# A fused attention and FFN kernel on one core: buffers relaid so that FFN weights lie over attention buffers, first FFN LayerNorm inside attention, wo over two banks, last tile in column pieces

## Chip, cores, metric

One Trainium2 chip, one of its cores. The metric is the device time of one execution of the program, in microseconds (us); the kernel before ran three times: 936.22, 937.30 and 937.99 us, median 937.3.

## What is computed

Two branches share a normalised input xn (2048 rows of 576), in bf16. Branch A is attention of 32 heads against a cached K and V of 16 heads (the last 512 positions of the cache). Branch B is a small mixer and an FFN. The result joins both.

```python
xn = layernorm(x)
q  = (xn @ wq)                       # 32 heads of 128
s  = softmax(q k^T / sqrt(128)) v @ wo
h  = gelu(layernorm(xn) @ w1)        # 576 to 576
x1 = xn + shifted(h) @ w2            # four column groups, shifted by +1 -1 +2 -2 rows
b  = x1 + gelu(layernorm(x1) @ w3) @ w4   # 576 to 4608 to 576
out = x + s * silu(b)
```

## The kernel before

The rows are split into four query blocks of 512. The first half of the program is the attention. It runs over 128 units, a unit being one head of one block. In the turn of unit u TensorE (PE) does four stages: `stage_q` (L268) projects q of unit u+1 over five chunks of 128 input columns, `stage_s` (L283) makes the scores of unit u in four chunks, whose exponentials ACT writes as pT (L285), `stage_v` (L298) multiplies pT of unit u-1 with v into two PSUM banks called po, from which VectorE (DVE) makes the reciprocal ri (L301) and the normalised o (L302), and `stage_t` (L309) has a DMA transpose on SP's queue turn o of unit u-2 into oT. The buffers of o are three (`o_pool`), those of oT 36.

Everything else is hung on unit numbers in a table `fill`: the output projection wo of the block before (`wo_units`, L325 for 512 columns of each row tile, L336 for the other 64 of all four tiles), the second LayerNorm (`ln2`) and its transposes (`tr2`, L239, into xnnT), the mixer's matmuls `b1` (L363) and `b2` (L399, result x1o by L404 and L410, stored to x1_dram by L411), the LayerNorm of the next block (`ln1`), loads of K and V (`load_kv`, L180 and L181) and of wq in pieces of four heads (`load_wq`, L175 and L177), and a check on the size of the scores. For the check DVE takes the largest absolute value of each K head (`k_max`, L256) and of each wq piece (L470, one reduction over 2560 columns), and `finish_flag` sends the maxima through a small DRAM tile mx_dram to one partition (L416 to L425). A branch at the end of the program would redo the attention in a safer form if the flag were set; it isn't taken. The last block's wo runs after the last unit, alone on PE, over the one bank of `ps_wo`.

The second half is the FFN. It loads x1 of a block (L519), normalises it (`ln3`: L116, L117, L95 to L105, L120, written to xm_b) and transposes it by DMA (L535) into x1nT; the weights w3 and w4 come in nine slices (`load_w`, L525 to L529, all of them tiles w_s in the profile). For each block of rows it runs 36 steps of `up` (L558, with the gelu on ACT at L561) and of `down` (L567 for 512 columns into one of four banks pm, L568 for 64 columns into pr). `finish` then makes the output of each of four tiles: bs (L576, L577), tanh (L579), g (L581, stored to g_dram by POOL at L582, which only the fallback branch reads), o (L584, L585) and the store (L586). The last block does all its ups first and then its downs tile by tile, so that three finishes lie beside matmuls.

The Python order of the calls isn't the order on each engine. A scheduler reorders independent instructions, so a load or a reduction may be issued long before its place in the program; `manual_schedule(engines=...)` and `keep_in_program_order` turn that off for the engines or instructions named. Each engine then runs its own list strictly in order, DMA issues included. SBUF is given out in stacks of pools: pools of the second half lie where pools of the first half lay, in order of their declaration, and a tile's first write waits until the readers of whatever lay there are done.

Of the kernel before, what the change touches and what calls it, by code (L numbers as in the profile page):

```python
# [8 lines left out]
P = 128  # L9
# [6 lines left out]
SP = mybir.EngineType.SP  # L16

# [10 lines left out]
def kernel(  # L28
# [94 lines left out]

    with ExitStack() as actx:
# [5 lines left out]
        wo_sb = res.tile([P, Hq, D], BF16, name="wo_sb")  # L130
# [4 lines left out]
        xnT_b = [res.tile([P, NDC, QB], BF16, name=f"xnT_b{i}") for i in range(2)]  # L135
        xnnT = res.tile([P, NDC, QB], BF16, name="xnnT")
        xn_b = [res.tile([P, TB, DP], BF16, name=f"xn_b{i}") for i in range(2)]
        xnn_b = res.tile([P, TB, DP], BF16, name="xnn_b")
        w1_sb = res.tile([P, NDC, 5 * P], BF16, name="w1_sb")
        w2_sb = res.tile([P, 5, D], BF16, name="w2_sb")  # L140
        mx = res.tile([P, 8 + Hkv], FP32, name="mx")
        gate = res.tile([1, 1], BF16, name="gate")

        oT_pool = pool("oT_pool", 36)
# [3 lines left out]
        o_pool = pool("o_pool", 3)  # L148
# [92 lines left out]
        def tr1_first():  # L241
            for kc, (cst, cw) in enumerate(DCH):
# [19 lines left out]
        def stage_q(u):  # L262
# [51 lines left out]
        def wo_units(qb):  # L314
            units = []
            st = {}
            for tt in range(TB):
                for h0 in range(0, Hq, 8):
                    def unit(tt=tt, h0=h0):
                        if tt == 0 and h0 == 0:  # L320
                            so_t[qb] = so_pool.tile([P, TB, D], BF16, name="s_out")
                        if h0 == 0:
                            st["ps"] = ps_wo.tile([P, M0], FP32, name="pswo", tag="wo")
# [7 lines left out]
            for tt in range(TB):  # L331
                def unit(tt=tt):
                    if tt == 0:
                        st["pr"] = ps_wo.tile([P, TB, R0], FP32, name="pswr", tag="wo")
# [46 lines left out]
        x1_t = {}  # L381

        def b2_shift(b):
# [6 lines left out]
            x1_t[b] = x1o_pool.tile([P, TB, D], BF16, name="x1o")  # L390
# [347 lines left out]
```

## Time and profile before

| | value |
|---|---|
| median of three runs | 937.3 us |
| the profiled execution's own time | 935.56 us |
| its span, first to last instruction | 933.7 us |
| mean granted TensorE clock | 0.982 |
| PE busy | 860.9 us (92%) |
| DVE, ACT, POOL busy | 376.5 (40%), 433.4 (46%), 46.0 (5%) us |
| DMA, mean over the span | 90 GB/s |

The span is read from left to right as follows: a start of some 12 us in which PE has nothing, the attention up to 577 us, the last block's wo to 611, a junction, and the FFN from 625 to the end. PE is the engine with the most work, so the places where PE stands still, and those where its granted clock is below full speed, are what an edit can win.

### The profile page before, as it was taken

How to read it: one execution, taken by the hardware profiler on the slowest of the kernel's cores; microseconds unless marked ns; L12 is line 12 of the kernel's file. 1: busy time of each engine (PE TensorE's matmuls, PEld its weight loads, DVE VectorE, ACT ScalarE, POOL GpSimd, SP SyncE). 2: the span in 40 equal slices, each digit the busy share in tenths (PEclk: the TensorE clock that was granted, in tenths of full speed). 3: DMA queues.
4: the chain of work that ended last, by engine and by line, in shares of the span. 5: the costliest groups of instructions: out<-in, count | busy, mean ns of one | idle time of the engine just before them, and what ended most of it. 6: DMA issues, size and time to landing. Idle time of an engine off the chain costs nothing.

```text
span 933.7 us, 15814 instructions
## 1 busy us (share of the span) xinstructions
PE 860.9 (92%) x6266; PEld 469.7 (50%) x6376; DVE 376.5 (40%) x1180; ACT 433.4 (46%) x812; POOL 46.0 (5%) x93
## 2 busy tenths in 40 slices
PE   4799889999969999999999999939999999999996
PEld 2455545554545465555465555424444444444453
DVE  7769763348743226563116543300306006003022
ACT  2556553366657247677247665013224224224510
POOL 1501200000000000000000000010000000000000
PEclk9999999999999999999999999979999999999998
DMA  8975952132463123274123234279105004101001
GB/s 183 208 169 138 196 107 55 53 90 60 104 118 91 37 69 88 58 153 113 16 69 86 60 86 106 87 224 311 30 1 148 9 1 127 29 1 51 0 15 41
DMA packets 162960, 83.72 MB, mean 90 GB/s; under 512 B 119488, under 2 KB 160704, under 8 KB 162880
## 3 DMA queue, kind: packets, MB, share of 16 engines
q1 hardware_dynamic: 159184, 72.16, 33.4%
q0 software_dynamic: 3408, 10.19, 4.1%
q8 instruction: 52, 0.85, 0.4%
q10 hardware_dynamic: 288, 0.30, 0.1%
q14 instruction: 28, 0.23, 0.1%
HBM read 47.07 MB, written 9.44 MB: 61 GB/s over the span
## 4 chain that ended last, share of the span: by engine, by line
PE 69%; issue 13%; ACT 9%; DMA 5%; DVE 3%; SPq 1%; POOL 0%; DVEq 0%; ACTq 0%; POOLq 0%
PE ph L558 16%; PE pm L567 13%; PE psq L268 11%; PE pswo L325 10%; PE po L298 7%; PE sc L283 6%; ACT qT L274 4%; ACT pT L285 4%; PE pr L568 2%; PE ph L363 2%; DMA oT<-o 2%; PE psx L399 1%; DMA kT<-in_A_k_cache_dram 1%; PE pswr L336 1%; DMA wq_b<-in_A_wq_dram 1%
## 5 line engine op out<-in xcount | busy, mean ns | idle before, releaser
L285 ACT ACTIVATE pT<-sc 128x512 bf16<-128x512 f32 x512 | 266.1, 607 | 58.1 <-PE sc L283 58.0
L558 PE MATMUL ph<-x1nT,w_s 128*128 128x512 bf16 x701 | 173.5, 383 | 15.1 <-DMA x1nT<-xm_b 14.0
L298 PEld LDWEIGHTS <-pT 128*128 128x128 bf16 x2048 | 140.9, 99 | 91.3 <-DVE o L302 27.1
L298 PE MATMUL po<-v_sb,pT 128*128 128x129 bf16 x2048 | 164.4, 222 | 21.3 <-DVE o L302 21.3
L561 ACT ACTIVATE h<-ph 128x512 bf16<-128x512 f32 x144 | 85.6, 596 | 171.7 <-PE ph L558 171.6
L283 PE MATMUL sc<-qT,kT 128*128 128x512 bf16 x512 | 153.4, 381 | 6.6 <-ACT pT L285 0.9
L268 PE MATMUL psq<-xnT_b,wq_b 128*128 128x512 bf16 x600 | 156.3, 386 | 2.3 <-issue 0.2
L567 PE MATMUL pm<-w_s,h 128*128 128x512 bf16 x557 | 152.2, 380 | 0.2
L301 DVE RECIPROCAL ri<-po 128x2 f32<-128x2 f32 x256 | 42.4, 167 | 194.5 <-PE po L298 193.3
L302 DVE TENSOR_TENSOR o<-po,ri 128x256 bf16<-128x256 f32 x256 | 107.5, 422 | 17.4 <-DMA oT<-o 11.2
L325 PE MATMUL pswo<-wo_sb,oT 128*128 128x512 bf16 x497 | 111.8, 379 | 2.8 <-ACT s_out L328 2.1
L558 PEld LDWEIGHTS <-w_s 128*128 128x128 bf16 x720 | 64.3, 99 | 89.4 <-DMA x1nT<-xm_b 14.1
L568 PE MATMUL pr<-w_s,h 128*128 128x64 bf16 x576 | 108.0, 193 | 1.0
L274 ACT ACTIVATE qT<-psq 128x512 bf16<-128x512 f32 x96 | 57.3, 597 | 78.3 <-PE psq L268 78.1
L576 DVE TENSOR_TENSOR bs<-pm,x 128x512 f32<-128x512 f32 x16 | 10.7, 687 | 204.8 <-PE pm L567 149.8
L567 PEld LDWEIGHTS <-h 128*128 128x128 bf16 x576 | 56.2, 98 | 67.3
L268 PEld LDWEIGHTS <-wq_b 128*128 128x128 bf16 x640 | 60.2, 99 | 58.6 <-issue 3.5
L325 PEld LDWEIGHTS <-oT 128*128 128x128 bf16 x512 | 49.4, 98 | 59.7 <-issue 2.9
L283 PEld LDWEIGHTS <-kT 128*128 128x128 bf16 x512 | 50.4, 99 | 46.2 <-issue 1.8
L568 PEld LDWEIGHTS <-h 128*128 128x128 bf16 x576 | 55.4, 98 | 12.7
L328 ACT ACTIVATE s_out<-pswo 128x512 bf16<-128x512 f32 x16 | 9.6, 597 | 105.4 <-PE pswo L325 105.4
L116 DVE BATCH_NORM_STATS2 ln_st<-x 128x6 f32<-128x288 bf16 x32 | 12.5, 431 | 71.9 <-DMA x<-x_dram 71.9
(83 smaller groups left out, 419.3 us busy)
## 6 DMA issues: line engine op xcount, KB each, us to landing
wq_b<-in_A_wq_dram SPq DMA_DIRECT2D x32, 512.0 KB, 3.9
w_s<-in_B_w_dram SPq DMA_DIRECT2D x9, 576.0 KB, 8.2
wo_sb<-in_A_wo_dram POOLq DMA_DIRECT2D x4, 1152.0 KB, 8.0
w_s<-in_B_w_dram SPq DMA_DIRECT2D x9, 512.0 KB, 8.4
s_dram<-s_out SPq DMA_DIRECT2D x4, 576.0 KB, 3.3
x_dram<-x1o SPq DMA_DIRECT2D x4, 576.0 KB, 3.3
s_b<-s_dram SPq DMA_DIRECT2D x4, 576.0 KB, 5.5
x_b<-in_A_x_dram SPq DMA_DIRECT2D x4, 576.0 KB, 6.3
```

The costliest lines, as they stand in the source:

```text
L268: nc.tensor.matmul(psq[:, :], lhsT=w[:, kc, hh * Dh:(hh + 1) * Dh], rhs=xnT_b[qb % 2][:, kc, :], start=(kc == 0), stop=(kc == NDC - 1))
L274: nc.scalar.activation(out=qT[:, :], in_=psq[:, :], func=ACT.Copy)
L283: nc.tensor.matmul(sc[:, :], lhsT=kT[:, g, kc * P:(kc + 1) * P], rhs=qT[:, :], start=True, stop=True)
L285: nc.scalar.activation(out=pT[:, :], in_=sc[:, :], func=ACT.Exp, scale=SCALE)
L298: nc.tensor.matmul(po[:, j, :], lhsT=pTs[kc][:, tt * P:(tt + 1) * P], rhs=v_sb[:, g, kc, 0:Dh + 1], start=(kc == 0), stop=(kc == KCH - 1))
L301: nc.vector.reciprocal(out=ri[:], in_=po[:, :, Dh])
L302: nc.vector.tensor_tensor(out=o[:, t0:t0 + 2, :], in0=po[:, :, 0:Dh], in1=ri[:].unsqueeze(2).to_broadcast([P, 2, Dh]), op=ALU.mult)
L325: nc.tensor.matmul(st["ps"][:, :], lhsT=oT_t[qb * Hq + h][:, tt, :], rhs=wo_sb[:, h, 0:M0], start=(h == 0), stop=(h == Hq - 1))
L558: nc.tensor.matmul(ph[:, :], lhsT=w3[:, kc, f0:f0 + P], rhs=x1nT[b % 2][:, kc, :], start=(kc == 0), stop=(kc == NDC - 1))
L561: nc.scalar.activation(out=h3[:, :], in_=ph[:, :], func=ACT.Gelu_apprx_tanh)
L567: nc.tensor.matmul(pm[tt][:, :], lhsT=lhsT, rhs=w4[:, fc % WS, 0:M0], start=(fc == 0), stop=(fc == FC - 1))
L568: nc.tensor.matmul(pr[:, tt, :], lhsT=lhsT, rhs=w4[:, fc % WS, M0:D], start=(fc == 0 and tt == 0), stop=(fc == FC - 1), skip_group_check=True)
```

## The change

There are five parts.

1. **Buffers.** xT_b (it takes the places of xnT_b and of x1nT), xn_b, xnn_b, the x1 buffers (now one pool of two for x1o and x1) and the small tiles move into pools that live through both halves. oT and wo_sb move to the end of the attention's stack. So the nine pairs of weight slices lie over kT, v_sb, wq_b, xnnT, w1, w2, mx, xraw, qT, pT, o and hb, and no longer over wo_sb.
2. **LN3 inside the attention.** The x1 load of block 0 is called at unit 106 (`3 * Hq + 10`), its LN3 at unit 123. With the buffers of part 1 the scheduler also moves block 1's x1 load and LN3 there.
3. **Order and the score check.** SP and POOL follow program order in the attention. k_max stays at its units in block 1; each wq maximum becomes five reductions of 512 columns, kept in program order. o has four buffers.
4. **Last wo.** The last block's wo takes its banks from ps_pq (two banks) and not from ps_wo (one); its store goes through ACT's queue.
5. **Finish.** o becomes (th + 1) * t1 with t1 = bs * s, so that g is off its path; g's store moves from POOL's to ACT's queue. The last tile is computed in three column pieces of 288, 192 and 96, each with a bank and a finish of its own.

The diff, cut to what the steps speak of:

```diff
+    keep = ctx.enter_context(tc.tile_pool(name="keep", bufs=1))
+    xT_b = [keep.tile([P, NDC, QB], BF16, name=f"xT_b{i}") for i in range(2)]
+    xn_b = [keep.tile([P, TB, DP], BF16, name=f"xn_b{i}") for i in range(2)]
+    xnn_b = keep.tile([P, TB, DP], BF16, name="xnn_b")
+    x1_pool = ctx.enter_context(tc.tile_pool(name="x1_pool", bufs=2))
...
+    def load_x1(b):
+        x1 = x1_pool.tile([P, TB, D], BF16, name="x1")
+        nc.sync.dma_start(out=x1[:], in_=rows(x1_dram, b * TB, TB))
...
         res = pool("a_res", 1)
-        wo_sb = res.tile([P, Hq, D], BF16, name="wo_sb")
         kT = res.tile([P, Hkv, W], BF16, name="kT")
...
-        oT_pool = pool("oT_pool", 36)
...
-        o_pool = pool("o_pool", 3)
+        o_pool = pool("o_pool", 4)
...
+        oT_pool = pool("oT_pool", 36)
+        wo_sb = pool("a_wo", 1).tile([P, Hq, D], BF16, name="wo_sb")
...
+        def wq_max(j, kc):
+            tc.keep_in_program_order(nc.vector.tensor_reduce(
+                out=mx[:, Hkv + NDC * j + kc:Hkv + NDC * j + kc + 1], in_=wq_b[j % NWQ][:, kc, :], axis=AX.X,
+                op=ALU.max, apply_absolute_value=True))
...
+            psp, tag = (ps_pq, "pq") if qb == NB - 1 else (ps_wo, "wo")
...
-                            st["ps"] = ps_wo.tile([P, M0], FP32, name="pswo", tag="wo")
+                            st["ps"] = psp.tile([P, M0], FP32, name="pswo", tag=tag)
...
-                        nc.sync.dma_start(out=rows(s_dram, qb * TB, TB), in_=so_t.pop(qb)[:])
+                        (nc.scalar if qb == NB - 1 else nc.sync).dma_start(out=rows(s_dram, qb * TB, TB),
+                                                                           in_=so_t.pop(qb)[:])
...
+            for kc in range(NDC):
+                at(Hq + 4 * j + (kc + 1) // 2, lambda j=j, kc=kc: wq_max(j, kc))
+        at(3 * Hq + 10, lambda: load_x1(0))
+        at(3 * Hq + 27, lambda: ln3(0))
...
+        with tc.manual_schedule(engines={SP, POOL}):
+            ln1(0)
...
-        load_x1(0)
-        load_w(0)
-        ln3(0)
-        for i in range(1, NSL):
+        for i in range(NSL):
             load_w(i)
...
-            nc.vector.scalar_tensor_tensor(out=g2[:], in0=th[:], scalar=1.0, in1=bs[:], op0=ALU.add, op1=ALU.mult)
-            nc.gpsimd.dma_start(out=g_dram[t * P:(t + 1) * P, :], in_=g2[:])
-            o = fin.tile([P, D], BF16, name="o")
-            nc.vector.tensor_tensor(out=o[:], in0=g2[:], in1=s_b[:, tt, :], op=ALU.mult)
-            nc.vector.tensor_tensor(out=o[:], in0=o[:], in1=x_b[:, tt, :], op=ALU.add)
-            nc.sync.dma_start(out=out2[t * P:(t + 1) * P, :], in_=o[:])
...
+                nc.vector.tensor_tensor(out=t1[:], in0=bs[:], in1=s_b[:, tt, lo:hi], op=ALU.mult)
+                o = fin.tile([P, n], BF16, name="o")
+                nc.vector.scalar_tensor_tensor(out=o[:], in0=th[:], scalar=1.0, in1=t1[:], op0=ALU.add, op1=ALU.mult)
+                nc.vector.tensor_tensor(out=o[:], in0=o[:], in1=x_b[:, tt, lo:hi], op=ALU.add)
+                nc.sync.dma_start(out=out2[t * P:(t + 1) * P, lo:hi], in_=o[:])
+                g2 = fin.tile([P, n], BF16, name="g2")
+                nc.vector.scalar_tensor_tensor(out=g2[:], in0=th[:], scalar=1.0, in1=bs[:], op0=ALU.add, op1=ALU.mult)
+                nc.scalar.dma_start(out=g_dram[t * P:(t + 1) * P, lo:hi], in_=g2[:])
...
+                cuts = [0, 288, 480, D]
+                for i in range(3):
+                    lo, hi = cuts[i], cuts[i + 1]
+                    ps = pm[TB - 1 - i][:, 0:hi - lo]
+                    for fc in range(FC):
+                        nc.tensor.matmul(ps, lhsT=h3_t[fc][:, tt * P:(tt + 1) * P],
+                                         rhs=w4_s[fc // WS][:, fc % WS, lo:hi], start=(fc == 0), stop=(fc == FC - 1))
+                    finish(b, tt, [([(ps, lo, hi)], lo, hi)])
```

The change moves more than these lines show. Three places stand here; a row is one instruction, or several of one kind with their count, in the order in which the engine runs them.

SP's queue early in block 0, before: loads of K and V for thirteen heads come first, and this is where they end and the first oT appears.

```order
L180 DMA_TRANSPOSE kT<-in_A_k_cache_dram 128x512
L181 DMA v_sb<-in_A_v_cache_dram 128x4x128
L180 DMA_TRANSPOSE kT<-in_A_k_cache_dram 128x512
L181 DMA v_sb<-in_A_v_cache_dram 128x4x128
L180 DMA_TRANSPOSE kT<-in_A_k_cache_dram 128x512
L175 DMA wq_b_76<-in_A_wq_dram 128x4x512
L309 DMA_TRANSPOSE oT<-o 128x4x128
L177 DMA wq_b_76<-in_A_wq_dram 64x512
L181 DMA v_sb<-in_A_v_cache_dram 128x4x128
```

The same queue in the changed kernel, from the load of the fourth head on (L196 and L197 are K and V, L330 is oT, L191 and L193 are wq):

```order
L196 DMA_TRANSPOSE kT<-in_A_k_cache_dram 128x512
L197 DMA v_sb<-in_A_v_cache_dram 128x4x128
L330 DMA_TRANSPOSE oT<-o 128x4x128 x2
L196 DMA_TRANSPOSE kT<-in_A_k_cache_dram 128x512
L197 DMA v_sb<-in_A_v_cache_dram 128x4x128
L330 DMA_TRANSPOSE oT<-o 128x4x128
L191 DMA wq_b_89<-in_A_wq_dram 128x4x512
L193 DMA wq_b_89<-in_A_wq_dram 64x512
L330 DMA_TRANSPOSE oT<-o 128x4x128
```

Before, the first oT stands behind nearly all loads of K and V; now the loads of one head stand between two of them.

SP's queue at the end of the attention, before (L309 is oT, L411 the store of x1o, L546 and L548 loads for finish, L519 the x1 load, L340 the store of the last s_out, L526 to L529 the weights, L535 the transposes of LN3's result):

```order
L411 DMA x_dram<-x1o 128x4x576
L309 DMA_TRANSPOSE oT<-o 128x4x128 x6
L546 DMA s_b<-s_dram 128x4x576
L548 DMA x_b<-in_A_x_dram 128x4x576
L546 DMA s_b<-s_dram 128x4x576
L548 DMA x_b<-in_A_x_dram 128x4x576
L519 DMA x_8974<-x_dram 128x4x576
L340 DMA s_dram<-s_out 128x4x576
L526 DMA w_s_8928<-in_B_w_dram 128x4x512
L528 DMA w_s_8928<-in_B_w_dram 64x512
L529 DMA w_s_8937<-in_B_w_dram 128x4x576
L526 DMA w_s_8929<-in_B_w_dram 128x4x512
```

And in the changed kernel (L434 is the store of x1 of a block, L143 the LN3 transposes, L136 an x1 load, L540 to L543 the weights):

```order
L434 DMA x_dram<-x_8147 128x4x576
L330 DMA_TRANSPOSE oT<-o 128x4x128
L143 DMA_TRANSPOSE xT_b_73<-xnn_b 128x5x128 x4
L330 DMA_TRANSPOSE oT<-o 128x4x128
L136 DMA x_9091<-x_dram 128x4x576
L330 DMA_TRANSPOSE oT<-o 128x4x128 x5
L143 DMA_TRANSPOSE xT_b_74<-xn_b_75 128x5x128
L540 DMA w_s_9015<-in_B_w_dram 128x4x512
L542 DMA w_s_9015<-in_B_w_dram 64x512
L543 DMA w_s_9016<-in_B_w_dram 128x4x576
```

The weights stood behind the store of the last s_out and now stand behind the last oT; four LN3 transposes and an x1 load stand among the last oT.

The new x1 load of block 0, on SP in the changed kernel, around unit 105 (L255 are the transposes of the mixer's input, x_7381 is x1 of block 0):

```order
L330 DMA_TRANSPOSE oT<-o 128x4x128
L255 DMA_TRANSPOSE xnnT<-xnn_b 128x5x128 x4
L330 DMA_TRANSPOSE oT<-o 128x4x128
L136 DMA x_7381<-x_dram 128x4x576
L330 DMA_TRANSPOSE oT<-o 128x4x128 x2
```

And the place on DVE where x_7381 is first read (L322 and L323 make ri and o, two pairs for a unit):

```order
L323 TENSOR_TENSOR o<-po,ri 128x256
L322 RECIPROCAL ri<-po 128x2
L323 TENSOR_TENSOR o<-po,ri 128x256
L322 RECIPROCAL ri<-po 128x2
L323 TENSOR_TENSOR o<-po,ri 128x256
L117 BN_STATS ln_st<-x_7381 128x6 x3
L322 RECIPROCAL ri<-po 128x2
L118 BN_AGGR ln_mv<-ln_st 128x2
L117 BN_STATS ln_st<-x_7381 128x6
L323 TENSOR_TENSOR o<-po,ri 128x256
```

Before, no instruction of LN3 stood on DVE before the last unit's o, and no x1 load on SP before the last oT. Now DVE's queue has LN3's first statistics between the o of two units, and SP's queue has the load behind an oT, four transposes and another oT.

## Rows read from the trace of the kernel before

**Rows 1.** Waits (engine, line, releaser; us in total, times, longest us).
```profile
PE po L298 <- DVE o L302: 21.3, 12, 4.1
...
PE ph L558 <- DMA x1nT<-xm_b: 14.0, 1, 14.0
...
DVE o L302 <- DMA oT<-o: 11.2, 6, 4.5
```

**Rows 2.** Costliest groups: VectorE (busy us, mean ns; idle before, by releaser).
```profile
L470 DVE TENSOR_REDUCE mx<-wq_b 128x1 f32<-128x2560 bf16 x8 | 22.6, 2820 | 18.2 <-DMA wq_b<-in_A_wq_dram 18.2
```

**Rows 3.** Windows (start:end, length, busy us by engine, granted clock, DMA share, GB/s).
```profile
40.00:60.00 20.00, 16.48 (x126) 9.76 (x126) 11.83 (x33) 9.59 (x19) 0.00 (x0) 0.91 0.98 203
260.00:280.00 20.00, 12.89 (x96) 7.75 (x96) 10.18 (x34) 9.67 (x19) 1.69 (x2) 0.91 0.61 104
626.00:630.00 4.00, 4.00 (x10) 1.49 (x10) 0.00 (x0) 0.97 (x2) 0.00 (x0) 0.51 1.01 334
```

**Rows 4.** Timeline of TensorE, end of wo and start of FFN (start, us).
```profile
607.29 3.89 PE L336 MATMUL pswr<-wo_sb,oT 128*128 128x64 bf16 x128 [0.69 <-ACT s_out L328]
625.17 0.59 PE L558 MATMUL ph<-x1nT,w_s 128*128 128x512 bf16 x1 [13.98 <-DMA x1nT<-xm_b]
625.97 6.02 PE L558 MATMUL ph<-x1nT,w_s 128*128 128x512 bf16 x18 [0.22 <-issue]
```

**Rows 5.** Timeline of SP's queue at the junction.
```profile
616.18 7.46 SPq L535 DMA_TRANSPOSE x1nT<-xm_b  x4
```

**Rows 6.** Timeline of VectorE, the first LayerNorm.
```profile
7.75 0.69 DVE L256 TENSOR_REDUCE mx<-kT 128x1 f32<-128x512 bf16 x1 [0.72 <-DMA kT<-in_A_k_cache_dram]
...
9.07 0.68 DVE L256 TENSOR_REDUCE mx<-kT 128x1 f32<-128x512 bf16 x1
```

**Rows 7.** SP's transposes by line: issue ns min/median/max, first and last start.
```profile
L309 SPq DMA_TRANSPOSE oT<-o x128: 1188/1191/2740, 28.6 to 577.6; - x128
...
L239 SPq DMA_TRANSPOSE xnnT<-xnn_b x16: 1201/1250/2787, 42.3 to 413.9; - x16
```

**Rows 8.** DMA issues (count, KB each, median us to landing).
```profile
w_s<-in_B_w_dram SPq DMA_DIRECT2D x9, 576.0 KB, 8.2
...
out_dram<-o SPq DMA_DIRECT2D x16, 144.0 KB, 1.9
```

**Rows 9.** Timeline of TensorE and VectorE at the first FFN block boundary.
```profile
701.64 4.48 PE L558 MATMUL ph<-x1nT,w_s 128*128 128x512 bf16 x20
...
705.96 0.59 PE L567 MATMUL pm<-w_s,h 128*128 128x512 bf16 x2
706.14 0.69 DVE L576 TENSOR_TENSOR bs<-pm,x 128x512 f32<-128x512 f32 x1
```

**Rows 10.** Timeline of SP's queue in block 0.
```profile
5.95 0.58 SPq L181 DMA_DIRECT2D v_sb<-in_A_v_cache_dram  x1
6.58 0.51 SPq L175 DMA_DIRECT2D wq_b<-in_A_wq_dram  x1
...
59.01 12.64 SPq L309 DMA_TRANSPOSE oT<-o  x4
```

**Rows 11.** Landing time of the x1 loads, line 519.
```profile
DMA to landing us min/median/max: 4.6/6.8/9.4
```

**Rows 12.** Costliest groups: VectorE's g and o in finish.
```profile
L581 DVE SCALAR_TENSOR_TENSOR g<-th,bs 128x576 bf16<-128x576 f32 x16 | 11.9, 756 | 5.4 <-ACT th L579 5.2
...
L584 DVE TENSOR_TENSOR o<-g,s_b 128x576 bf16<-128x576 bf16 x16 | 7.0, 455 | 0.2
```

**Rows 13.** Timeline of the last tile, all engines.
```profile
924.47 0.19 PE L568 MATMUL pr<-w_s,h 128*128 128x64 bf16 x1
924.67 0.69 DVE L576 TENSOR_TENSOR bs<-pm,x 128x512 f32<-128x512 f32 x1 [5.45 <-PE pr L568]
925.28 0.21 DVE L577 TENSOR_TENSOR bs<-pr,x 128x64 f32<-128x64 f32 x1
...
928.07 0.33 SPq L586 DMA_DIRECT2D out_dram<-o  x1
```

More of the change, by code (lines that the diff above doesn't have):

```diff
@@ L16 @@
 SP = mybir.EngineType.SP
+POOL = mybir.EngineType.Pool
 LN_EPS = 1e-5
@@ L403, in b2 @@
             b2_mm(ps[:, :], b, tt, 0, M0)
-            nc.vector.tensor_tensor(out=x1_t[b][:, tt, 0:M0], in0=ps[:, :], in1=xn_t[b][:, tt, 0:M0], op=ALU.add)
+            nc.vector.tensor_tensor(out=x1o_t[b][:, tt, 0:M0], in0=ps[:, :], in1=xn_t[b][:, tt, 0:M0], op=ALU.add)
         def b2_rem(b):
@@ L409, in b2_rem @@
                 b2_mm(ps[:, tt, :], b, tt, M0, D)
-            nc.vector.tensor_tensor(out=x1_t[b][:, :, M0:D], in0=ps[:, :, :], in1=xn_t[b][:, :, M0:D], op=ALU.add)
-            nc.sync.dma_start(out=rows(x1_dram, b * TB, TB), in_=x1_t.pop(b)[:])
+            nc.vector.tensor_tensor(out=x1o_t[b][:, :, M0:D], in0=ps[:, :, :], in1=xn_t[b][:, :, M0:D], op=ALU.add)
+            nc.sync.dma_start(out=rows(x1_dram, b * TB, TB), in_=x1o_t.pop(b)[:])
             xn_t.pop(b)
@@ L499 @@
         NSL = FC // WS
[L500 to L504 removed]
+        w3_s, w4_s = [], []
+        for i in range(NSL):
+            w3_s.append(res.tile([P, NDC, WS * P], BF16, name=f"w3_s{i}"))
+            w4_s.append(res.tile([P, WS, D], BF16, name=f"w4_s{i}"))
         h3_pool = pool("h3_pool", 6)
@@ L508 @@
         sx_pool = pool("sx_pool", 2)
-        small = pool("b_small", 4)
         ps_h3 = pool("ps_h3", 3, PSUM)
         ps_h2 = pool("ps_h2", 1, PSUM)
-        for w in xm_b:
-            nc.gpsimd.memset(w[:, :, D:], 0.0)
-        x1_t = {}
-        def load_x1(b):
-            x1 = x1_pool.tile([P, TB, D], BF16, name="x1")
-            nc.sync.dma_start(out=x1[:], in_=rows(x1_dram, b * TB, TB))
-            x1_t[b] = x1
         def load_w(i):
@@ L529, in load_w @@
             nc.sync.dma_start(out=w4[:], in_=B_w4[c0:c0 + WS * P, :].rearrange("(fc p) d -> p fc d", p=P))
-        def ln3(b):
-            xm = xm_b[b % 2]
-            layernorm(small, [xm[:, tt, 0:D] for tt in range(TB)], [x1_t[b][:, tt, :] for tt in range(TB)])
-            for tt in range(TB):
-                nc.sync.dma_start(out=x1nT[b % 2][:, :, tt * P:(tt + 1) * P], in_=xm[:, tt, :], transpose=True)
-        load_x1(0)
-        load_w(0)
-        ln3(0)
-        for i in range(1, NSL):
+        for i in range(NSL):
             load_w(i)
@@ new lines, in finish @@
+            for ps, lo, hi in parts:
+                n = hi - lo
+                bs = fin.tile([P, n], FP32, name="bs")
+                for src, l0, l1 in ps:
+                    nc.vector.tensor_tensor(out=bs[:, l0 - lo:l1 - lo], in0=src, in1=x1_t[b][:, tt, l0:l1], op=ALU.add)
+                th = fin.tile([P, n], FP32, name="th")
+                nc.scalar.activation(out=th[:], in_=bs[:], func=ACT.Tanh, scale=0.5)
+                t1 = fin.tile([P, n], FP32, name="t1")
+                nc.vector.tensor_tensor(out=t1[:], in0=bs[:], in1=s_b[:, tt, lo:hi], op=ALU.mult)
[6 more added lines that the diff above has]
+                nc.scalar.dma_start(out=g_dram[t * P:(t + 1) * P, lo:hi], in_=g2[:])
@@ L605 @@
                 for tt in range(TB):
-                    finish(b, tt, pm, pr)
+                    finish(b, tt, whole(tt))
             else:
```

92 lines of the change are left out of this document (41 added, 51 removed).

## Prediction

> **What bounds the kernel now.** I read the waits first, since TensorE (PE) does nearly all the work and what counts is where it stands still. In [rows 1] the reader sees two large standstills: 14.0 us before the first FFN matmul, which waits for the transposed LN3 output, and 21.3 us in 12 waits of the attention's po matmuls for DVE's o. Behind the o stand DVE's own waits: 11.2 us for oT transposes, which free o's buffers, and in [rows 2] 18.2 us before the eight reductions of wq, of 2.82 us each. DVE runs its instructions in order, so whatever it waits for, the next o waits too.
>
> Next the windows [rows 3]. The granted clock drops around these stalls: four stretches of 20 us stand at 0.91 of full speed (the first and the last are shown; 100 to 120 and 120 to 140 read the same), and the first four us of the FFN at 0.51, about the lower of TensorE's two levels (1.2 of 2.4 GHz). So a stall costs its own length and some matmuls at half speed.
>
> Last the timelines of the junction [rows 4, 5] and of both ends. The profiled execution took 935.56 us; the median of the runs, 937.3, is 1.7 above. I sum against 935.56 and add 1.7 at the end.
>
> **The change, part by part.**
>
> *Start.* Two reductions over kT of 0.69 and 0.68 stand inside the first LayerNorm, one after a wait of 0.72 [rows 6]; program order puts them into block 1. Together 2.1; neighbours on DVE overlap by about 0.1 each, and the small operations then keep their own spacing: -1.8. In block 1 they stand where DVE has room or not: see (2).
>
> *Junction.* Before, the weights' buffers lay on wo_sb, which the wo matmuls read until 607.29 + 3.89 = 611.2 [rows 4]. Only then SP issues weights and, between them, four transposes of 7.46 us in all [rows 5], and PE starts at 625.17 after a gap of 13.98, with another of 0.22. Now the weights lie on kT, v, wq and other buffers that the last unit is the last to read; its oT starts at 577.6 [rows 7]. Nine slices are 10.4 MB; at the 334 GB/s of [rows 3] they take 31 us and are there at about 609. PE needs the first alone, 8.2 us after its issue [rows 8], at about 586. The transposes of x1 are issued inside the attention. So 13.98 + 0.22 go. The clock: 20 up matmuls took 625.17 to 631.99, 6.8 us, and 20 later ones 4.3 (4.48 with the last one's end, [rows 9]): 2.5 go. The last wo over two banks removes four waits of 0.69 (the last of them stands in [rows 4]): 2.8. I leave 0.2 for a restart. The last s_dram store costs nothing on ACT: it waits for ACT's own result, and its reader comes blocks later. Sum: -19.3.
>
> *Attention, what goes.* The 21.3 us of [rows 1] have causes that the change addresses: oT queued on SP behind hoisted kT and v loads, reductions that wait for wq, the maximum's small DMA. The pieces stand behind wq's landing, SP keeps program order, and o has a fourth buffer. The four clock drops are (1 - 0.91) x 20 = 1.8 each, 7.2. Together 28.5.
>
> *Attention, what comes.* (1) Block 0: a wq load now stands on SP behind four xnnT transposes, 5.0 us at the median of 1.25, more if one takes 2.79 [rows 7], while a unit lasts 3.1 (12.64 for four, [rows 10]). Between 0 and 4; I take 2.5. (2) Block 1: sixteen kT reductions and forty of wq share DVE with LN, b1 and b2: between 0 and 3, I take 1. (3) **Unit 106 is a new wait.** DVE's LN3 statistics of block 0 stand there, and the x1 load that they need stands on SP behind an oT, four xnnT transposes (5.0 and more) and another oT. Counted from the o that both queues share, the load is issued at about 8 and lands 4.6 to 6.8 later [rows 11], at 12.6 to 14.8; DVE is there after two more units' o, at about 6.2. It stands at least 6.4; PE has two po banks and some 4 us of other work ahead of it, so it loses about 2.6, and 1.4 more from DVE's crowd in units 107 to 109, where b1 stands too: between 0 and 6, I take 4. (4) Unit 125: LN3 of block 1 waits for its x1 load, which stands behind the store of x1 and four LN3 transposes of block 0 (5.0 again): between 0 and 5, I take 3. The oT behind those transposes come 5 us late, which four o buffers (12 us) cover. (5) Clock: at most one drop of 1.8 behind each of these; between 0 and 5, I take 2. Sum 12.5. Net in the attention: -28.5 + 12.5 = -16.0.
>
> *FFN, the three block boundaries.* Each tile's finish gains an operation: t1 = bs*s in fp32, then o from th and t1, besides g. 576 columns take 0.455 with bf16 inputs and 0.756 with fp32 inputs [rows 12]. t1 mixes both: between these ends I take 0.756, the row of the operation that has an fp32 operand. A tile then costs DVE 0.9 for bs, three times 0.756, and 0.455: 3.6, where it cost 2.6. PE wants the third tile's bank about when bs(2) starts (pm at 705.96, bs at 706.14, [rows 9]), so there is no slack. Two finishes stand before bs(2); t1 hides in the wait for tanh, so bs(2) comes about 1.4 later; PE has five up matmuls (1.1 us) put in front of it. Between 0 and 1.5 per boundary, I take 0.8, three times: +2.5. ACT issues g's store and waits for g there, with the next Gelu behind it; that is inside this range. POOL loses those stores.
>
> The Trainium skill (VectorE: DVE Perf Modes, the perf-mode tier table) says that tensor_tensor runs at twice the plain rate with bf16 inputs in SBUF and at the plain rate with fp32; that speaks against this rewrite. The two durations agree with it. By it t1 costs the 0.756 taken; at the bf16 price this term would be about 1.5 and not 2.5.
>
> *Tail.* From the last matmul's end, 924.66, to the issue of the last store, 928.07, are 3.4 us of bs, tanh, g, o and o over 576 columns [rows 13]. Now the last piece has 96 columns and g is off the chain: five operations of 0.2 to 0.3, an estimate from the 0.21 for 64 columns [rows 13], and the gaps make about 1.4: -2.0. Three column pieces instead of two cost about 0.1 on PE. After the last store's landing, 1.9 after its issue [rows 8], some 3.7 us pass to the span's end at 933.7, in which no row stands; POOL's stores of g may be behind them, and they are gone. Between 0 and -3.7, I take -1.9. Sum: -3.8.
>
> **Sum:** -1.8 - 19.3 - 16.0 + 2.5 - 3.8 = -38.4. 935.56 becomes 897.2, and the median, 1.7 above, 899.
>
> **The rivals.**
>
> *All waits stay hidden.* The x1 loads arrive in time and SP keeps up; only 2.5 of the 12.5 comes: 10 less, 889. For it: oT came late only where transfers were crowded. Against it: DVE's order, in which LN3 stands some 6 us ahead of its load.
>
> *The new waits are big.* DVE's stalls at both places reach the whole o ring, and (1), (3), (4), (5) come to their ends, 4 + 6 + 5 + 5 = 20 in place of 11.5, with the boundaries at 4.5 in place of 2.5: 10.5 more, 909; with (2) at its end too 911. For it: the old stalls had a clock drop beside them [rows 3].
>
> *The weights still wait for wo.* If one buffer under them is read late, or all are released with the whole attention, PE waits for a slice's landing, 8.2 [rows 8], plus some cold clock: 9 to 10 of the junction come back, 908. Against it: in the order the weights' issues stand right behind the last oT, with no store between.
>
> *Slower: SP paces the attention.* A DMA transpose holds SP for its issue time d. In block 0 a unit needs one oT, half a kT and half a v (0.58), and a quarter of wq's two issues (0.51 each, [rows 10]): d + (d + 0.68)/2 + 0.3 = 1.5 d + 0.64 with gaps. At 1.19 [rows 7] that is 2.4, under the unit's 3.1; at 1.6 it is the unit. To eat the 38 us in 32 units it must be 1.2 over the unit, 4.3, so d = 2.4: from there the change loses. At d = 2.9 block 0 takes 5.0 per unit, 61 us more: 899 + 61 = 960. For it: single issues took 2.74 and 2.79 [rows 7]. Against it: the median of 128 is 1.19.
>
> **How the numbers follow.** The forecast has 0.56, all hidden 0.20, big waits 0.15, weights late 0.06, slower 0.03. The range: low, all hidden with no cost at the boundaries and the tail's better end, 889 - 2.5 - 1.8 = 885; high, the big waits with the tail's poor end and the start's gain lost, 911 + 1.9 + 1.8 = 914. The slower case is left out. A measurement of this kernel can tell about 0.2%, 1.9 us, from no change; no case but the last, and a sum of mishaps beyond the high end, lies above 935: faster 0.96, same 0.01, slower 0.03.
>
> **What would show it.** Right: the first matmul near 10.5; no wait of ph for the transposes, the first up matmul directly behind the last wo matmul near 590, at a granted clock of 1.00; no wait of pswo for s_out; one or two waits of DVE's ln_st for x of 3 to 7 us in block 3 with po behind them; gaps before pm at the boundaries below 1.5; the last store issued 1.4 after the last matmul. Wrong: po waits for o over 20 us in sum, a gap over 5 at the junction, weights issued after wo, transposes with a median issue above 1.6.

## Result and the profile after

The changed kernel takes 906.69 us (median of four runs, 906.21 to 907.03), the kernel before 937.64 (936.22 to 939.65, four runs); ratio 0.9668, 95% interval 0.9649 to 0.9687. The forecast was 899, in a range of 885 to 914. Direction and range hold; 8 us of the forecast gain didn't come. The profiled execution took 906.96 us with a span of 905.1 (before 935.56 and 933.7), so the spans differ by 28.6 where the sum said 38.4.

Cut at the first psq matmul, the last po matmul, the first up matmul and the last matmul of the FFN, as the timelines of TensorE have them:

| stage | before | after | difference | forecast |
|---|---|---|---|---|
| start, to the first psq | 14.53 | 12.72 | -1.8 | -1.8 |
| attention, to the end of the last po | 562.35 | 557.08 | -5.3 | -16.0 |
| wo and junction, to the first up | 48.29 | 30.55 | -17.7 | -16.8 |
| FFN, to its last matmul | 299.49 | 297.24 | -2.3 | -2.5 clock, +2.5 boundaries |
| tail, to the end of the span | 9.04 | 7.53 | -1.5 | -3.8 |

The waits (engine, line, releaser; us in total, times, longest) that answer to [rows 1]:

```profile
DVE ln_st L117 <- DMA x<-x_dram: 14.6, 4, 6.5
...
PE po L319 <- DVE o L323: 7.0, 2, 3.6
...
PE psq L289 <- DMA wq_b<-in_A_wq_dram: 6.0, 3, 3.7
```

The wait of ph for the transposes and the twelve waits of po for a late o are gone. Two other waits of po stand in their place, and two kinds are new: psq for wq, which the kernel before didn't have, and DVE for x in the attention, where two of its four stand. The windows (TensorE's clock is the third number from the end, then the DMA share and GB/s) answer to [rows 3]:

```profile
40.00:60.00 20.00, 19.54 (x152) 11.48 (x152) 13.58 (x37) 12.08 (x24) 1.06 (x2) 1.00 1.22 223
80.00:100.00 20.00, 16.11 (x122) 9.30 (x124) 14.90 (x61) 10.32 (x20) 5.28 (x11) 0.91 1.10 213
100.00:120.00 20.00, 17.70 (x129) 10.15 (x130) 13.40 (x51) 10.57 (x21) 0.24 (x1) 0.91 0.89 185
480.00:500.00 20.00, 16.27 (x106) 8.91 (x106) 15.45 (x62) 10.45 (x21) 0.00 (x0) 0.91 0.35 88
560.00:580.00 20.00, 16.79 (x94) 9.27 (x96) 11.92 (x44) 3.14 (x6) 4.35 (x9) 0.83 0.43 83
600.00:604.00 4.00, 3.95 (x34) 2.02 (x32) 0.00 (x0) 2.93 (x5) 0.00 (x0) 1.00 1.09 334
```

The FFN now starts at full clock, but four windows of the attention stand below it, as before, three of them at other places. Reckoned as in the prediction they lose (3 x 0.09 + 0.17) x 20 = 8.8 us.

TensorE at the two late loads of wq, at the two late places of the attention and at the end of wo, the last against [rows 4]:

```profile
94.94 2.31 PE L289 MATMUL psq<-xT_b,wq_b 128*128 128x512 bf16 x5 [3.67 <-DMA wq_b<-in_A_wq_dram]
...
110.73 1.78 PE L289 MATMUL psq<-xT_b,wq_b 128*128 128x512 bf16 x5 [2.12 <-DMA wq_b<-in_A_wq_dram]
...
486.46 0.76 PE L319 MATMUL po<-v_sb,pT 128*128 128x129 bf16 x8 [3.33 <-DVE o L323]
...
562.86 1.05 PE L319 MATMUL po<-v_sb,pT 128*128 128x129 bf16 x8 [3.64 <-DVE o L323]
...
596.62 3.90 PE L358 MATMUL pswr<-wo_sb,oT 128*128 128x64 bf16 x128
600.35 2.97 PE L564 MATMUL ph<-xT_b,w_s 128*128 128x512 bf16 x12
```

The first up starts while the last wo matmul is still draining: the gap of 13.98 is nil, and no 0.69 stands in front of pswr. SP and DVE around unit 106:

```profile
473.01 5.25 SPq L255 DMA_TRANSPOSE xnnT<-xnn_b  x4
478.37 1.20 SPq L330 DMA_TRANSPOSE oT<-o  x1
479.62 0.59 SPq L136 DMA_DIRECT2D x<-x_dram  x1
```

```profile
477.47 0.42 DVE L323 TENSOR_TENSOR o<-po,ri 128x256 bf16<-128x256 f32 x1
484.40 1.18 DVE L117 BATCH_NORM_STATS2 ln_st<-x 128x6 f32<-128x288 bf16 x3 [6.51 <-DMA x<-x_dram]
...
561.59 0.46 DVE L117 BATCH_NORM_STATS2 ln_st<-x 128x6 f32<-128x288 bf16 x1 [5.24 <-DMA x<-x_dram]
```

That is the chain that the prediction drew for unit 106: four transposes of 5.25 ahead of the load, the load at 479.62, DVE standing 6.51, PE behind it 3.33. The last line is the same wait at unit 125, where PE stands 3.64.

### The profile page after: what moved, and what is told of

The parts are those of the page before. It is cut to its first block, busy times and chain, and to the rows that moved or that the text cites. A ratio compares the mean times of both kernels' runs of the same rounds, so it can differ in the third digit from the quotient of the medians.

```text
span 905.1 us, 15932 instructions
## 1 busy us (share of the span) xinstructions
PE 859.1 (95%) x6304; PEld 473.4 (52%) x6412; DVE 394.4 (44%) x1237; ACT 433.6 (48%) x814; POOL 36.9 (4%) x75
## 4 chain that ended last, share of the span: by engine, by line
## 5 line engine op out<-in xcount | busy, mean ns | idle before, releaser
L564 PE MATMUL ph<-xT_b,w_s 128*128 128x512 bf16 x701 | 171.0, 380 | 0.9
L289 PE MATMUL psq<-xT_b,wq_b 128*128 128x512 bf16 x600 | 154.2, 384 | 8.1 <-DMA wq_b<-in_A_wq_dram 6.0
L573 PE MATMUL pm<-w_s,h 128*128 128x512 bf16 x523 | 143.4, 380 | 0.1
L322 DVE RECIPROCAL ri<-po 128x2 f32<-128x2 f32 x256 | 42.7, 167 | 184.3 <-PE po L319 182.9
L584 DVE TENSOR_TENSOR bs<-pm,x 128x512 f32<-128x512 f32 (+3 forms) x18 | 11.1, 633 | 251.5 <-PE pm L573 203.6
L323 DVE TENSOR_TENSOR o<-po,ri 128x256 bf16<-128x256 f32 x256 | 108.0, 422 | 6.4 <-DVE ri L322 0.3
L574 PE MATMUL pr<-w_s,h 128*128 128x64 bf16 x540 | 99.2, 193 | 0.8
L573 PEld LDWEIGHTS <-h 128*128 128x128 bf16 x540 | 52.6, 98 | 63.7 <-issue 0.6
L574 PEld LDWEIGHTS <-h 128*128 128x128 bf16 x540 | 51.1, 98 | 12.2 <-issue 0.4
L586 ACT ACTIVATE th<-bs 128x576 f32<-128x576 f32 (+3 forms) x18 | 11.0, 626 | 44.5 <-DVE bs L584 44.5
```

Source lines behind the costliest of these rows:

```text
L322: nc.vector.reciprocal(out=ri[:], in_=po[:, :, Dh])
L323: nc.vector.tensor_tensor(out=o[:, t0:t0 + 2, :], in0=po[:, :, 0:Dh], in1=ri[:].unsqueeze(2).to_broadcast([P, 2, Dh]), op=ALU.mult)
L564: nc.tensor.matmul(ph[:, :], lhsT=w3[:, kc, f0:f0 + P], rhs=xT_b[b % 2][:, kc, :], start=(kc == 0), stop=(kc == NDC - 1))
L573: nc.tensor.matmul(pm[tt][:, :], lhsT=lhsT, rhs=w4[:, fc % WS, 0:M0], start=(fc == 0), stop=(fc == FC - 1))
L574: nc.tensor.matmul(pr[:, tt, :], lhsT=lhsT, rhs=w4[:, fc % WS, M0:D], start=(fc == 0 and tt == 0), stop=(fc == FC - 1), skip_group_check=True)
```

## Experiments

All runs are edits of the changed kernel, each beside the kernel before on the same chip. "Attention" is the stretch of the table above in the profiled execution (562.4 before).

| run | median us (lowest to highest) | ratio to before, 95% | attention |
|---|---|---|---|
| the change | 906.69 (906.21 to 907.03) | 0.9668, 0.9649 to 0.9687 | 557.1 |
| the change again | 906.59 (903.97 to 909.85) | 0.9702, 0.9663 to 0.9742 | 554.8 |
| x1 load early | 902.27 (900.12 to 906.31) | 0.9642, 0.9596 to 0.9688 | 552.2 |
| LN3 of block 1 late | 902.45 (900.11 to 903.16) | 0.9638, 0.9603 to 0.9674 | 550.1 |
| wq one unit early | 904.28 (901.96 to 915.2) | 0.9694, 0.9625 to 0.9764 | 552.7 |
| LN3 behind the attention | 895.72 (894.46 to 897.11) | 0.9563, 0.9526 to 0.9600 | 545.6 |
| and wq two units early | 900.23 (897.00 to 901.93) | 0.9607, 0.9571 to 0.9644 | 550.9 |
| and w2 later | 891.77 (888.57 to 898.96) | 0.9554, 0.9501 to 0.9607 | 539.1 |
| and wo loads spread | 890.24 (887.09 to 896.16) | 0.9539, 0.9494 to 0.9585 | 537.6 |
| wo_sb first | 914.39 (912.21 to 917.25) | 0.9779, 0.9738 to 0.9819 | 556.1 |
| free order | 899.61 (897.94 to 900.53) | 0.9606, 0.9574 to 0.9639 | 551.9 |
| LN3 behind, free order | 896.33 (892.65 to 898.44) | 0.9575, 0.9537 to 0.9613 | 547.8 |
| last tile whole | 908.29 (907.85 to 910.28) | 0.9709, 0.9683 to 0.9736 | 559.2 |

The change run a second time scatters over 6 us, so a difference under 3 between two rows is read as nothing more than that.

> The change itself, unedited, to have it on the same chip as the three that follow: 906.7 within 2, or lower by what the kernel before is lower here.

**The x1 load eight units earlier.**

```diff
-        at(3 * Hq + 10, lambda: load_x1(0))
+        at(3 * Hq + 2, lambda: load_x1(0))
```

> The x1 load of block 0 is called eight units earlier (unit 98), ahead of the xnnT transposes on SP; all else as in the change. Theory A (a late load stops DVE, PE stops 3.3 us behind it, and one clock drop of 1.7 us follows): DVE's wait for x at 484 and the gap of 3.33 in po go, no window below 1.00 there; 906.7 - 5.0 = 901.7, between 901 and 903. Rival B (the place is crowded with DVE work or transfers, the wait only moves to the next operation): a gain under 2, 905 or more.

902.27, a profiled span 5.2 below the change's, so theory A in size. DVE's wait for x now stands at 424, 3.59 long, with no stall of PE behind it, and the window 480 to 500 is at 1.00. In place of the gap of 3.33 there is one of 1.71 at 478, and its cause is another one:

```profile
474.22 0.43 DVE L121 TENSOR_SCALAR xnn_b<-x,ln_mv,nr_y 128x576 bf16<-128x576 bf16 x1 [0.90 <-DMA xnnT<-xnn_b]
```

DVE's LN3 writes its result into xnn_b, the buffer that the four xnnT transposes are still reading. It stands 0.85 to 0.94 before each of four such writes, and the next o waits behind them. So a part of rival B holds too: some of the wait moved to the next operation.

**LN3 of blocks 1 to 3 in program order on DVE** (`keep_in_program_order` on its bn_stats).

```diff
-                nc.vector.bn_stats(out=st[:, j, :], in_=src[:, j * hw:(j + 1) * hw])
+                ins = nc.vector.bn_stats(out=st[:, j, :], in_=src[:, j * hw:(j + 1) * hw])
+                if keep_order:
+                    tc.keep_in_program_order(ins)
```

> LN3 of blocks 1 to 3 is kept in program order on DVE, so that LN3 of block 1 leaves the last units and runs in the FFN. Theory A: DVE's wait of 5.24 for x near 561 and PE's gap of 3.64 go, and with it the drops at 560 to 572 (0.74, 0.50, 0.91: 3.4 us lost at most, 1.7 at least): 906.7 - 5.3 to 7.0, so 899.7 to 901.4. Rival B (PE would stand there for something else, such as oT or the last softmax): a gain under 2. Rival C: LN3 of block 1 comes too late for its ups in the FFN, a gap of ph at the first block boundary: nothing gained.

902.45, span 6.8 lower. The gap near 559 is gone, the window 560 to 580 at 1.00, and TensorE enters the FFN with no gap: theory A, with a median 1 us above its range. The gap near 483 is still there with 3.15 and its window reads 1.00 this time, so not every stall is followed by a drop.

**wq one unit earlier in block 0, ahead of that unit's other calls.**

```diff
-            at(4 * (j - 1), lambda j=j: load_wq(j))
+            if j <= 8:
+                fill.setdefault(4 * (j - 1) - 1, []).insert(0, lambda j=j: load_wq(j))
+            else:
+                at(4 * (j - 1), lambda j=j: load_wq(j))
```

> In block 0 the wq loads are called one unit earlier and ahead of that unit's K and V loads. Theory A (SP's program order makes wq late): the psq waits of 3.67 and 2.12 and the two clock drops behind them (0.91 in both windows, 3.4 us) go: 906.7 - 9.2 = 897.5, between 896 and 900. Rival B (the transfers themselves are slow there, DMA share 1.1 to 1.36, a landing of 7.0 against 4.0): the loads land late all the same, at most one of the two gaps goes: 903 or more.

904.28 with a wide scatter, and one of the two gaps gone: what rival B said, but not for its reason. The first wq gap is gone; the second is 2.44 now, behind a wq load that SP issued at 101.99, after LN1's four transposes of 6.14. That load landed in 4.2, the usual time, so here it was late by its place on SP.

**LN3 behind the attention.** x1 and LN3 of block 0 are called where the kernel before calls them, and LN3's bn_stats keep program order; buffers as changed.

```diff
-        at(3 * Hq + 10, lambda: load_x1(0))
-        at(3 * Hq + 27, lambda: ln3(0))
...
-        for i in range(NSL):
+        load_x1(0)
+        load_w(0)
+        ln3(0)
+        for i in range(1, NSL):
             load_w(i)
```

with `keep_order=True` for every block in the edit above.

> The buffers stay relaid, but LN3 of every block is kept in program order on DVE and x1 and LN3 of block 0 are called behind the attention as before. Theory A (the relaid buffers alone win the junction, LN3 inside the attention is a loss): both stalls of DVE for x go, 3.33 + 3.64 + 3.4 to 5.1 of clock: 894.6 to 896.3; LN3 and its transposes end near 588, beside wo that ends near 593, and ph has no gap over 1. Rival C (LN3 inside the attention is what closes the junction): the transposes stand behind weights on SP and land after wo's end, PE waits 3 to 10 for them with a cold clock: 900 to 908.

895.72: theory A, 11 better than the change. The junction stays shut (TensorE, end of wo and start of FFN):

```profile
576.71 8.80 PE L350 MATMUL pswo<-wo_sb,oT 128*128 128x512 bf16 x40
585.35 3.90 PE L361 MATMUL pswr<-wo_sb,oT 128*128 128x64 bf16 x128
589.08 3.19 PE L568 MATMUL ph<-xT_b,w_s 128*128 128x512 bf16 x13
```

and SP issues LN3's transposes between weights, long before that:

```profile
566.08 5.17 SPq L146 DMA_TRANSPOSE xT_b<-xnn_b  x4
```

So LN3 inside the attention, one of the change's parts, wins nothing at the junction: the 18 us between the end of these issues and the first up were room enough. It costs what its two stalls and the clock drops behind them cost.

**wo_sb first.** The buffers' part undone for the first slices.

```diff
         res = pool("a_res", 1)
+        wo_sb = res.tile([P, Hq, D], BF16, name="wo_sb")
         kT = res.tile([P, Hkv, W], BF16, name="kT")
...
-        wo_sb = pool("a_wo", 1).tile([P, Hq, D], BF16, name="wo_sb")
```

> The change with wo_sb put back to the front of the attention's buffers, so that the first four weight slices lie over it again; LN3, the order and the rest stay as changed. Theory A (the buffers' place closes the junction): the first weights are issued only when wo ends near 600, PE waits for the landing of one slice, 4 to 8, and 2.5 of cold clock follow: 906.7 + 6.5 to 10.5 = 913 to 917. Rival C (LN3's transposes inside the attention close it): the gap stays below 2, 909 or less.

914.39: theory A. SP issues the first weight only when wo is done, and PE waits 4.31 and starts slowly (its FFN takes 299.72, 2.5 more than the change's):

```profile
599.55 0.38 SPq L540 DMA_DIRECT2D w_s<-in_B_w_dram  x1
```

```profile
595.62 3.90 PE L358 MATMUL pswr<-wo_sb,oT 128*128 128x64 bf16 x128
603.83 6.54 PE L564 MATMUL ph<-xT_b,w_s 128*128 128x512 bf16 x18 [4.31 <-DMA w_s<-in_B_w_dram]
```

The rest of the 13.98 of before went with the four transposes and the s_out store that no longer stand there. One thing stays untested: no run puts the store of the last s_out back on SP's queue, ahead of the weights, so how much of the junction hangs on that move is not shown.

**Free order.** SP and POOL without `manual_schedule`.

```diff
-        with tc.manual_schedule(engines={SP, POOL}):
+        with ExitStack():
             ln1(0)
```

> The change without program order for SP and POOL in the attention: the scheduler puts ten K loads ahead of the first oT again; o keeps its four buffers. Theory D (program order takes away oT's lateness in block 0 and makes wq late instead, one for the other): 906.7 within 4. Rival E (program order on SP is what won in the attention): po waits for o over 9 us in block 0 as before, 912 or more.

899.61: neither theory. Free order is 7 better than the change. In block 0 it brings back the oT that is late behind K and V, and later the wait for the flag of the score check (both on DVE):

```profile
46.34 0.43 DVE L323 TENSOR_TENSOR o<-po,ri 128x256 bf16<-128x256 f32 x1 [6.89 <-DMA oT<-o]
```

```profile
279.52 0.41 DVE L445 TENSOR_REDUCE mm<-m 1x2 f32<-1x256 f32 x1 [5.35 <-DMA m<-mx_dram]
```

PE loses 5.39 and 3.72 there. But wq's gaps shrink to 0.5 each, and the scheduler moves block 0's x1 load and LN3 ahead, so that the 3.33 is gone. To take the two apart:

> LN3 behind the attention as in the run that gave 895.7, and SP and POOL without program order. Theory D (the free order won 7 in the change only because it also loads x1 early; for the rest it puts oT's lateness and the flag's wait, 5.4 + 3.7, in place of wq's 3.5 + 1.7 with their clock drops): 895.7 within 3. Rival F (program order itself costs): 891 or less.

This is the run of LN3 behind the attention (the edits above) with free order added: 896.33 against 895.72, theory D. With the x1 stalls out of the way, program order and the scheduler's order are worth the same within the scatter; the change's program order traded one set of waits for another.

**wq two units earlier**, on top of LN3 behind the attention.

```diff
-                fill.setdefault(4 * (j - 1) - 1, []).insert(0, lambda j=j: load_wq(j))
+                fill.setdefault(4 * (j - 1) - 2, []).insert(0, lambda j=j: load_wq(j))
```

> As the run with LN3 behind the attention (895.7), and in block 0 each wq load is called two units earlier and ahead of K, V and LN1's transposes of that unit. Theory A (SP's order makes wq late): the two psq waits of 3.48 and 1.72 and the clock drops (0.87 and 0.96 in their windows, 3.4 us) go: 895.7 - 8.6 = 887, between 886 and 890. Rival B (the transfers are slow there whatever the order): 893 or more.

900.23, worse than without it: theory A falls, though psq's waits for wq are gone, and B has the number but not the reason. Now LN1's four transposes stand behind wq, and just there POOL issues a wo load:

```profile
100.60 11.49 SPq L258 DMA_TRANSPOSE xT_b<-xn_b  x4
```

```profile
100.39 0.93 POOL L230 DMA_DIRECT2D wo_sb<-in_A_wo_dram  x1 [0.31 <-issue]
```

Four transposes held SP for 11.49, the oT behind them came late, and po lost 5.57; another 3.96 went at 52, to b1 waiting for xnnT. The wo load wasn't alone: the last of w2's eight loads landed at 100.15, and a wq load issued at 99.40 was still under way.

**And w2 at unit 36**, then **and the wo loads at units 5, 13, 18 and 27**.

```diff
-        at(20, lambda: late(pT_t[20][0][0:1, 0:1], load_w2))
+        at(36, lambda: late(pT_t[36][0][0:1, 0:1], load_w2))
```

```diff
-            at(5 + 6 * i, lambda i=i: late(pT_t[5 + 6 * i][0][0:1, 0:1], lambda: load_wo(i)))
+            uw = (5, 13, 18, 27)[i]
+            at(uw, lambda i=i, uw=uw: late(pT_t[uw][0][0:1, 0:1], lambda: load_wo(i)))
```

> As the run before it in this call, and POOL's loads of w2 (eight transfers, needed in block 1 only) are called at unit 36 and not at unit 20. Theory A (order on SP): within 1 of the run before it. Rival B (the crowd of transfers at 80 to 110, DMA share 1.1 to 1.36): 2 to 4 better than it, and the landings of wq near 90 go from 6 to 7 down to 4.

> LN3 behind the attention, wq two units early, w2 at unit 36, and the four wo loads at units 5, 13, 18 and 27 and not 5, 11, 17 and 23, so that none starts next to the four xnnT or LN1 transposes. Theory B (a wo load of 1152 KB in flight holds up SP's transposes, 11.5 for four at 100 with wo landing after 12.4): no set of four over 7 in block 0, 888 within 2, and its runs lie within 4 of each other where the run with wo at the old units had 888.6 to 899.0. Rival A (only SP's order matters): 891.8 within 1, with the same scatter.

891.77 and 890.24: the first is 8 better than the run before it, more than the 2 to 4 that rival B had said, and wq near 94 lands in 4.2. In the second no wo load is issued beside the transposes and the four take their usual time:

```profile
94.24 5.18 SPq L258 DMA_TRANSPOSE xT_b<-xn_b  x4
```

In the run with w2 alone they took longer, with a wo load issued 0.15 after the first:

```profile
95.29 7.29 SPq L258 DMA_TRANSPOSE xT_b<-xn_b  x4
```

For these four of block 0 the runs line up: 5.2 with no wo load in flight at their start (also in the run of LN3 behind the attention, where the load follows 4.2 later), 6.1 with one issued 0.5 later (wq one unit early), 7.3 and 11.5 with one issued within 0.2. The wo load isn't the whole cause. Between 7.3 and 11.5 the wo load is the same, and what differs most is that w2's loads are out of the way. In block 1 of the run with spread wo loads four xnnT transposes took 6.13 with no wo load anywhere near, and in [rows 5] four took 7.46 among weights that SP itself had issued. What the spread wo loads add in time isn't resolved: 1.5 between the medians, and the scatter of 9 us that B said would go stays. Against the kernel before, this version has the lowest ratio (0.9539, attention 24.7 shorter); against the run with LN3 behind the attention alone the intervals overlap.

**The last tile whole**, as the three before it.

```diff
-                for tt in range(TB - 1):
+                for tt in range(TB):
                     for fc in range(FC):
                         down(pm, pr, fc, tt)
                     finish(b, tt, whole(tt))
...
```

> The change with the last tile computed whole, as the three tiles before it, and not in three column pieces. Theory H (the shorter last piece saves 1.4 of the chain after the last matmul, but its narrow store takes 1.07 to issue against 0.33 and 2.8 to land against 1.9): within 1 of the change itself in this call, and the last store lands about 1.9 after its issue. Rival G (the pieces are worth their 2.0): 1.5 to 2.5 slower than the change itself.

908.29 against 906.59, which is inside the scatter, so the medians don't decide between the theories. In the profile the last store is issued 3.59 after the last matmul, where the change has 1.43: the 2.0 that the pieces were to win at this place are there. The tail, from the last matmul to the end of the span, is 8.76, and between 6.3 and 8.5 (7.3 in the mean) in the twelve profiles with pieces. So at the end of the span some 1.4 of it are left, as far as one profile of the whole tile can tell. The profiled execution of this run lost 4.88 at 107 to wq besides, which has nothing to do with its edit.

## Why the prediction was right, and where it was wrong

**Start: right**, 1.8 of 1.8. **Junction: right**, and in the main for its reason. [Rows 4] had the 13.98 and the last of four waits of 0.69; all are gone, and the first 20 ups, which ran cold, take 2.3 less. Weights over wo_sb bring some 7 of it back (4.31 of gap and 2.5 of clock in the profile, 7.7 between the medians). That the transposes of x1 are issued inside the attention, which the prediction counted among the causes, wasn't needed. Gap, banks and clock together gave 20.0 (17.7 of the table, and 2.3 of the FFN) against 19.3.

**Attention: the step that failed.** What goes was right: the twelve waits of po for o, 21.3, are gone, and with them the clock drops behind them (the window 100 to 120 is low again, but its drop now stands behind a wait for wq). What comes was sized at 12.5 and measured 24.3 (waits of PE of 15.5, the 7.0 of po among them, and 8.8 of clock), so 28.5 less 24.3 is 4.2; the table has 5.3, since 1.1 of small waits of PE outside po went too. By its parts: (3) unit 106, taken as 4, measured 3.33; (4) unit 125, taken as 3, measured 3.64, with DVE's wait of 5.24 for x behind it; (2) block 1, taken as 1, 0.7. (3) and (4) were right in mechanism and place. (1) block 0, "between 0 and 4; I take 2.5", measured 3.67 + 2.12 = 5.8, outside its bounds, and its mechanism holds in part. Behind the four xnnT transposes (45.34 to 50.54) no wq load came late. The load behind the 2.12 stood behind four transposes, those of LN1. The load behind the 3.67 stood behind none, as SP's queue shows:

```profile
84.87 2.88 SPq L330 DMA_TRANSPOSE oT<-o  x1
87.85 0.53 SPq L191 DMA_DIRECT2D wq_b<-in_A_wq_dram  x1
```

It was issued behind one slow oT, and psq got it at 94.94, 7.1 later, while w2's eight loads were under way; the median landing is 4.0. PE was ready at 91.27, so at that median it would have lost 0.6 (an estimate), and slow transfers, which had no term, made the rest. Some 2 us of small waits had no term either; the longest, 1.33 before b1 at 339, has no releaser in the profile. (5) the clock, "at most one drop of 1.8 behind each of these; between 0 and 5, I take 2", measured 8.8. That is the largest error: a drop came with each of the four stalls, the last of about double length (0.83 in 560 to 580). The trace of before could have warned: its single stalls of 3.07, 2.71 and 4.14 had a window at 0.91 with them, and one of 2.74 had none. The rival of the big waits, whose (1), (3), (4) and (5) sum to 20, was nearer: these four measured 21.6. It was right on the clock and on block 0, both of which passed even their ends, and not on longer stalls at units 106 and 125.

**FFN boundaries: too dear.** +2.5 was taken (three times 0.8 is 2.4), and about 0.1 came: from the first up to the first pm the FFN took 6.66 before and takes 4.32 now, 2.34 less, and the whole FFN is 2.26 shorter. Here are DVE's third bs and TensorE at the first boundary:

```profile
676.76 0.75 DVE L590 SCALAR_TENSOR_TENSOR o<-th,t 128x576 bf16<-128x576 f32 x1
677.43 0.75 DVE L588 TENSOR_TENSOR t<-bs,s_b 128x576 f32<-128x576 f32 x1
...
680.17 0.69 DVE L584 TENSOR_TENSOR bs<-pm,x 128x512 f32<-128x512 f32 x1
```

```profile
674.70 4.26 PE L564 MATMUL ph<-xT_b,w_s 128*128 128x512 bf16 x19
678.80 0.60 PE L573 MATMUL pm<-w_s,h 128*128 128x512 bf16 x2
679.23 1.24 PE L564 MATMUL ph<-xT_b,w_s 128*128 128x512 bf16 x5
```

t1, a tensor_tensor with one fp32 operand, and o take 0.75 each, the price taken from [rows 12], and bs(2) comes 1.37 after the second block's first pm (680.17 - 678.80), where in [rows 9] it came 0.18 after (706.14 - 705.96): 1.2 later, near the 1.4 that was said. PE shows no gap: the five ups of 1.1 that the prediction had named, with one pair of pm after another, cover it. The lateness was right and the cover was under-counted.

**Tail: too hopeful by 2.3.** The chain after the last matmul went as sized, 1.4 from 897.59 to the end of the last add at 898.99. The other 1.9, for the 3.7 us after the last landing, didn't come. The last add on DVE and ACT's store of g beside it:

```profile
898.79 0.20 DVE L591 TENSOR_TENSOR o<-o,x_b 128x96 bf16<-128x96 bf16 x1
898.90 0.37 ACTq L595 DMA_DIRECT2D g_dram<-g  x1
```

and, by line (issue min/median/max in ns) and by size (KB, us to landing):

```profile
L592 SPq DMA_DIRECT2D out_dram<-o x18: 332/333/1071, 678.6 to 899.0; - x18
```

```profile
out_dram<-o SPq DMA_DIRECT2D x1, 24.0 KB, 2.8
```

ACT issues its store of g 0.12 before SP its store of o, whose issue at 899.0 is the one that takes 1.07 (0.33 in [rows 13]) and which lands 2.8 after its start (1.9 in [rows 8]). That is 0.9 back in this execution; in the second profile of the change the issue takes 0.61, the store lands in 1.9, and the tail is as long, 7.55. ACT's store isn't what decides it: it stands there in all twelve profiles with pieces, and the issue takes from 0.33 (in three of them) to 1.30. From the last landing to the end of the span there are 3.3 us in the first profile of the change, 4.3 in the second, 2.1 to 5.2 in all runs (3.3 in the mean), 3.7 before. POOL's store, which is gone, was not what they were, and what they are stays open.

**The rivals.** That the weights still wait for wo is out, and wo_sb first shows what it would have been. SP pacing the attention is out: the median issue of oT's transposes is 1.20, against the 2.4 from which it decides:

```profile
L330 SPq DMA_TRANSPOSE oT<-o x128: 1188/1198/2878, 22.7 to 570.5; - x128
```

That all waits stay hidden, at 889, is near what the kernel does (890 to 892) once LN3 is behind the attention and the loads of block 0 no longer meet.

**Luck.** The boundaries came 2.4 cheaper and the tail 2.3 dearer than forecast, and the two errors cancel. What the spans miss of the forecast, 9.8, is in size the attention's error of 10.7, less 0.7 that the junction gave over its forecast. The medians miss only 8, because the profiled execution of before was 1.7 below its median and that of the change is 0.3 above.

Left open: why some stalls of 3 us have a clock drop behind them and one (483 in the run with LN3 of block 1 late) has none. No run undoes the second wo bank, the fourth o buffer, the place of the score check or the new finish by itself; what they are worth is read from the waits alone.

## What to carry to other kernels

Where buffers are reused across two phases, put the early-dead ones under the data that the next phase loads first: with that, the gap at the junction stayed shut whether the next phase's LayerNorm stood early or late, and some 16 us of the 31 are this gap and the cold start behind it. Whether it does so with a store that waits for the last result ahead of the loads on their queue is not shown. Work pulled from a later phase into a busy one must find its data there already: here the load stood behind four transposes on the same queue, DVE's next o stood behind the operation that waited for it (6.51), and PE stood behind that o (3.33). Left beside the last projection, the same work cost PE no wait. Count clock drops with the stalls when summing a gain, and look at what else is in flight where a queue of transposes stands.

## What the runs showed of the hardware

Four DMA transposes that take 5.2 us to issue took 11.5 when a load of 1152 KB from another engine's queue was issued 0.2 us earlier, just behind eight smaller ones, and 7.3 when it followed 0.15 after, without those eight. The first of the four landed 12.1 and 6.3 us after its issue, against 3.5 in the run with spread wo loads, where the four took 5.2. The Trainium skill (DMA: Bandwidth & Descriptors, Issuing engines are not separate DMA queues) says that transfers run on the same 16 engines whichever engine starts them. These three runs agree, and they show in addition that the issue of a transpose itself takes longer on its queue while other loads are in flight, up to 5.28 us for one. A store of 96 columns (24 KB) took between 0.33 and 1.30 us to issue in twelve profiles, with another engine's store issued just ahead of it in each.
